# Issuing the first x load of a 2:4 sparse matmul from the ScalarE queue instead of the SyncE queue

## The chip, the cores and the metric

The kernel runs on one core of a Trainium2 chip. The metric is the device time of one execution in microseconds, the median over the runs shown.

## The reference

x has 16 x 512 = 8192 token rows of 1024 values, w is 1024 x 1024, b has 1024 values, all bf16. The rows of w are taken in groups of four along the contraction dimension. In each group and column the two entries of largest magnitude stay and the others become zero (2:4 sparsity); ties at the threshold stay.

```python
G = D // M                                  # M = 4, N = 2
wg = w.reshape(G, M, D)
mag = jnp.abs(wg)
order = jnp.argsort(mag, 1)
thr = jnp.take_along_axis(mag, order[:, M - N:M - N + 1, :], 1)
mask = (mag >= thr).astype(w.dtype)
wp = (wg * mask).reshape(D, D)
return jnp.einsum("bsd,df->bsf", x, wp) + b
```

## The kernel before

The 8192 tokens are 64 tiles of 128. The kernel has two stages.

In the first stage w comes in packed: partition q holds the four rows of group q, so that a group lies in one partition and the mask is elementwise work (`Piece`, L141 to L178: magnitudes, pairwise maxima and minima, threshold, mask, product). w is cut into six pieces (L124): half g of the contraction dimension and a column range. Pieces 0 and 1 are g = 0, columns 0 to 255 and 256 to 511. Since the rows are packed this way, x has to be split the same way, and TensorE transposes it: tiles 0 to 6 of x come in as halves of the contraction dimension ("a" for g = 0, "b" for g = 1), each is transposed in four steps against an identity (`transpose`, L189), and ScalarE copies the result from PSUM to SBUF (`copy_xt`, L198). Then TensorE multiplies with the pruned pieces as they are done (`mm_piece`, L209). The pruned weights also go to a scratch in DRAM and come back in natural row order (`save` L180, `reload` L183).

In the second stage tiles 7 to 63 are loaded with a transposing DMA in batches (`load_batch`, L240) and multiplied with the natural weights (L358 to L403).

The order of work in the first stage is written out by hand, one list per engine (L252 to L268). On TensorE it begins with fillers, matmuls on a tile of zeros whose results are not used: `filler(6, 4)` with 512 columns and `filler(8)` with 128 columns (L342, L343). Then come T6a (transpose tile 6, half a), F5 (five fillers), T5a, T4a, F6, T3a, T2a, F7, M5.0y (tile 5 with the second half of piece 0), and so on; M6.3 is tile 6 with piece 3. Each engine takes its list strictly in order. On VectorE the list is abs0, hi0, lo0, ..., mask0y, mask0x, mult0y, abs1, mult0x, ...: the steps of piece 0, then 1, 3, 2, 4, 5; `mult` is the last step of a piece. On ScalarE it is C6a, C5a, C4a, C2a, C3a, C6b, C1a, abs3, ...: the copies of the transposes, and the magnitudes of later pieces.

The loads of w, x and the bias stand at L104 to L121, all issued from SP in this order: the weights of piece 0 (256 KB), tile 6 half a (128 KB), tiles 4 and 5 half a (256 KB), tiles 2 and 3 half a, the weights of piece 1, and ten more. They run through `issue` (L90), so their instructions have line 92. Between the first two of these calls stands an activation on the tile of zeros (`spark`, L106), whose result is not used; with it the activation table is loaded (ACT_TABLE_LOAD, put there by the compiler).

Of the kernel before, what the change touches and what calls it, by code (L numbers as in the profile page):

```python
# [10 lines left out]
def kernel(  # L11
# [7 lines left out]
    nc = tc.nc  # L19
# [5 lines left out]
    Act = mybir.ActivationFunctionType  # L25
# [35 lines left out]
    def seq(eng, inst):  # L61
        if eng in tails:
            tc.add_manual_dep(inst.ins, tails[eng].ins.name, NOSYNC, reason="program order")
        tails[eng] = inst
        return inst
# [7 lines left out]
    def act(i):  # L73
        return seq("act", i)
# [4 lines left out]
    zeros = const.tile([P, P], bf16)  # L79
    dve(nc.vector.memset(zeros[:], 0.0))  # L80
    spark = const.tile([P, P], bf16)
# [8 lines left out]
    def issue(eng, out_, in_):  # L90
        q = nc.sync if eng == "sp" else nc.scalar
        return seq(eng, q.dma_start(out_, in_))  # L92

    def load_w(g, c0, c1, eng="sp"):
        issue(eng, w_sb[:, g, :, c0:c1], wv[:, g, :, c0:c1])

    def load_x(ta, tb, g, eng="sp"):
        xs = const.tile([P, tb - ta, HK], bf16, name=f"x_{ta}_{g}")
        issue(eng, xs[:], xv[:, ta:tb, g * HK:(g + 1) * HK])
        for t in range(ta, tb):  # L100
            x_sb[(t, g)] = xs[:, t - ta, :]


    load_w(0, 0, 256)  # L104
    for _ in range(1):
        act(nc.scalar.activation(spark[:], zeros[:], Act.Abs))  # L106
    load_x(6, 7, 0)
    load_x(4, 6, 0)
    load_x(2, 4, 0)
    load_w(0, 256, 512)  # L110
# [323 lines left out]
```

## Time and profile before

| | |
|---|---|
| time, median of 4 runs | 236.05 us |
| the four runs | 237.59, 235.97, 235.91, 236.14 us |
| the profiled execution | 237.59 us, of which the span is 235.8 us and 1.79 us lie around it |
| TensorE matmul busy | 230.0 us, 98% of the span |
| VectorE busy | 104.3 us, 44% |
| ScalarE busy | 15.3 us, 7% |
| second stage, matmuls of L395 | 800, 175.4 us, mean 379 ns |
| first stage, matmuls of L220 | 166, 25.4 us |
| transposes L195, fillers L132 | 56 and 32 matmuls, 5.7 and 6.1 us |
| granted TensorE clock in the records | 1.00 |

How to read it: PE is TensorE's matmuls, PEld its weight loads, DVE is VectorE, ACT ScalarE, SPq and ACTq the queues of DMAs that these engines issue. Times count from the start of the span. Matmuls are pipelined, so the duration of one (379 ns) is longer than the spacing of two (219 ns for 512 columns in the second stage). A bracket behind a timeline entry gives the idle time of the engine ahead of it and what ended that. "To landing" is the time from a DMA's issue until its data are there.

### The profile page before, as it was taken

Reading aid. Unit: us, or ns where it says so; the run is one execution under the profiler, and the core shown is the slowest. Engines: PE = TensorE matmul, PEld = TensorE weight load, DVE = VectorE, ACT = ScalarE, POOL = GpSimd, SP = SyncE. Lnnn points to the kernel's source line nnn. Section 1 sums busy time; section 2 is a strip of 40 time slices with the busy share of each in tenths; the row PEclk is TensorE's granted clock in tenths of the full one; section 3 lists DMA queues with packets and bytes.
Section 4 is the critical chain, followed back from the end, with each engine's and each line's share of the span. In section 5 each row is a group of like instructions: output and inputs, shape, how many; then the busy total and the mean of one; then the engine's idle time right before and its main releaser. Section 6 shows DMA issues by size and latency. Waiting matters only on the chain.

```text
span 235.8 us, 2851 instructions
## 1 busy us (share of the span) xinstructions
PE 230.0 (98%) x1164; PEld 114.4 (48%) x1184; DVE 104.3 (44%) x177; ACT 15.3 (7%) x27; POOL 0.7 (0%) x6
## 2 busy tenths in 40 slices
PE   7899999999999999999999999999999999999995
PEld 4899444444444444444444444444444444444443
DVE  3779839733424433432442343344244334324424
ACT  3288300000000000000000000000000000000000
POOL 1000000000000000000000000000000000000000
DMA  5995988999999992794129912496211221222122
GB/s 161 312 328 138 276 304 197 274 268 278 229 320 213 295 246 90 167 258 157 57 76 232 299 50 89 102 283 195 90 74 61 89 92 44 89 89 84 52 89 89
DMA packets 79500, 40.29 MB, mean 171 GB/s; under 512 B 60416, under 2 KB 71936, under 8 KB 79488
## 3 DMA queue, kind: packets, MB, share of 16 engines
q1 hardware_dynamic: 68352, 22.45, 43.6%
q10 hardware_dynamic: 11136, 17.67, 21.8%
q8 instruction: 9, 0.15, 0.3%
q14 instruction: 3, 0.02, 0.0%
HBM read 6.29 MB, written 18.87 MB: 107 GB/s over the span
## 4 chain that ended last, share of the span: by engine, by line
PE 96%; DMA 2%; issue 1%; SPq 1%; DVE 0%
PE ps L395 74%; PE ps L220 10%; PE ps L360 9%; DMA x<-in_x_dram 2%; PE tp L195 2%; PE ps L132 1%; SPq L92 1%; DVE o L364 0%
## 5 line engine op out<-in xcount | busy, mean ns | idle before, releaser
L395 PE MATMUL ps<-wp_nat,xb 128*128 128x512 bf16 x800 | 175.4, 379 | 0.8
L395 PEld LDWEIGHTS <-xb 128*128 128x128 bf16 x816 | 79.8, 98 | 96.3
L364 DVE TENSOR_TENSOR o<-ps,bias_sb 128x512 bf16<-128x512 f32 (+1 forms) x116 | 74.0, 676 | 117.2 <-PE ps L395 106.5
L220 PE MATMUL ps<-wp,xt 128*128 128x256 bf16 (+1 forms) x166 | 25.4, 308 | 0.1
L360 PE MATMUL ps<-wp_nat,xb 128*128 128x512 bf16 (+2 forms) x110 | 21.0, 348 | 0.1
L220 PEld LDWEIGHTS <-xt 128*128 128x128 bf16 x168 | 16.2, 98 | 7.5
L360 PEld LDWEIGHTS <-xb 128*128 128x128 bf16 x112 | 10.4, 98 | 10.7
L132 PE MATMUL ps<-zeros 128*128 128x128 bf16 (+1 forms) x32 | 6.1, 372 | 1.0 <-DVE zeros L80 1.0
L234 DVE TENSOR_TENSOR o<-ps,bias_sb 128x512 bf16<-128x512 f32 x7 | 4.8, 685 | 5.0 <-PE ps L220 5.0
L195 PE MATMUL tp<-ident,x 128*128 128x128 bf16 x56 | 5.7, 252 | 1.1 <-DMA x<-in_x_dram 1.1
L155 ACT ACTIVATE mag<-w_sb 128x1024 bf16<-128x1024 bf16 (+1 forms) x4 | 6.0, 1493 | 0.0
L200 ACT COPY xt<-tp 128x256 f32<-128x256 f32 x14 | 5.0, 373 | 9.2 <-PE tp L195 9.2
L195 PEld LDWEIGHTS <-x 128*128 128x128 bf16 x56 | 4.7, 124 | 1.5 <-DMA x<-in_x_dram 1.4
L152 DVE TENSOR_TENSOR wp<-w_sb,mag 128x1024 bf16<-128x1024 bf16 (+2 forms) x7 | 5.4, 766 | 0.2
L152 DVE TENSOR_TENSOR mag<-mag,hi 128x1024 bf16<-128x1024 bf16 (+2 forms) x7 | 5.3, 767 | 0.2
L132 PEld LDWEIGHTS <-zeros 128*128 128x128 bf16 x32 | 3.7, 147 | 2.6 <-issue 1.7
L235 DVE TENSOR_TENSOR o<-st,bias_sb 128x512 bf16<-128x512 f32 x7 | 4.8, 679 | 0.0
L152 DVE TENSOR_TENSOR lo<-mag 128x512 bf16<-128x512 bf16 (+1 forms) x6 | 3.0, 508 | 1.4 <-ACT mag L155 1.4
L229 ACT COPY st<-ps 128x512 f32<-128x512 f32 x7 | 3.6, 611 | 0.2 <-PE ps L220 0.2
L152 DVE TENSOR_TENSOR hi<-mag 128x512 bf16<-128x512 bf16 (+1 forms) x6 | 3.0, 507 | 0.0
L162 DVE TENSOR_SCALAR mag<-w_sb 128x1024 uint16<-128x1024 uint16 x2 | 0.9, 427 | 4.1 <-DMA w_sb<-in_w_dram 4.1
L152 DVE TENSOR_TENSOR hi<-hi,lo 128x256 bf16<-128x256 bf16 (+1 forms) x6 | 2.0, 337 | 0.2
(11 smaller groups left out, 6.5 us busy)
## 6 DMA issues: line engine op xcount, KB each, us to landing
out_dram<-o ACTq DMA_DIRECT2D x58, 256.0 KB, 4.1
wp_nat<-wp_scratch SPq DMA_DIRECT2D x2, 1024.0 KB, 6.4
x<-in_x_dram SPq DMA_DIRECT2D x5, 256.0 KB, 5.2
out_dram<-o ACTq DMA_DIRECT2D x10, 128.0 KB, 1.7
w_sb<-in_w_dram SPq DMA_DIRECT2D x4, 256.0 KB, 4.9
w_sb<-in_w_dram SPq DMA_DIRECT2D x2, 512.0 KB, 6.3
wp_scratch<-wp SPq DMA_DIRECT2D x4, 256.0 KB, 5.1
wp_scratch<-wp ACTq DMA_DIRECT2D x2, 512.0 KB, 5.0
```

The costliest lines, as they stand in the source:

```text
L132: pe(nc.tensor.matmul(warm_ps[:, :rep * P], lhsT=zeros[:], rhs=zeros[:, None, :].to_broadcast([P, rep, P]), start=True, stop=True))
L152: dve(nc.vector.tensor_tensor(out, a, b_, op=op))
L155: act(nc.scalar.activation(self.mag[:], self.w, Act.Abs))
L195: pe(nc.tensor.transpose(tp[:, m, :], xg[:, m, :], ident[:]))
L200: act(nc.scalar.copy(xt[:].bitcast(fp32), xpk[(t, g)][:].bitcast(fp32)))
L220: pe(nc.tensor.matmul(ps[:, c0 - h * FH:c1 - h * FH], lhsT=xpk[(t, g)][m], rhs=wp[:, g, m, c0:c1], start=(new and m == ms.start), stop=(le ...
L229: act(nc.scalar.copy(st[:], ps_open.pop((t, 0))[:]))
L234: dve(nc.vector.tensor_tensor(o[:, FH:], ps_open.pop((t, 1))[:], bias_sb[:, FH:], op=Alu.add))
L235: dve(nc.vector.tensor_tensor(o[:, :FH], staged.pop(t)[:], bias_sb[:, :FH], op=Alu.add))
L360: pe(nc.tensor.matmul(ps, lhsT=xt[:, kt, :], rhs=wp_nat[:, kt, c0:c1], start=(kt == 0), stop=(kt == KT - 1)))
L364: dve(nc.vector.tensor_tensor(o[:, c0:c1], ps, bias_sb[:, c0:c1], op=Alu.add))
L395: pe(nc.tensor.matmul(pss[h][:], lhsT=xt[:, kt, :], rhs=wp_nat[:, kt, h * FH:(h + 1) * FH], start=(kt == 0), stop=(kt == KT - 1)))
```

## The change

Three lines at the head of the loads. The load of tile 6, half a, is issued from ScalarE's queue and not from SP's, and it stands ahead of the activation, so that on ScalarE it is the first instruction, ahead of the table load. The activation works on one column instead of 128. The loop around it, which ran once, is gone. On SP all following loads stand one place further ahead; nothing else moves on any engine.

```diff
     load_w(0, 0, 256)
-    for _ in range(1):
-        act(nc.scalar.activation(spark[:], zeros[:], Act.Abs))
-    load_x(6, 7, 0)
+    load_x(6, 7, 0, "act")
+    act(nc.scalar.activation(spark[:, :1], zeros[:, :1], Act.Abs))
     load_x(4, 6, 0)
     load_x(2, 4, 0)
     load_w(0, 256, 512)
```

## The prediction

> **What bounds the kernel now.** I read the chain of waits first, since it says which engine the end hangs on. Its columns are start, length and what; times are us from the start of the span.
>
> ```profile
> 1.48 0.60 SPq L92
> 2.08 0.06 issue
> 2.13 4.46 DMA x<-in_x_dram
> 6.60 0.05 issue
> 6.64 1.04 PE tp L195 x8
> 7.68 0.64 PE ps L132 x6
> 8.32 0.85 PE tp L195 x8
> 9.18 0.75 PE ps L132 x7
> 9.92 1.34 PE ps L220 x12
> 11.26 0.45 PE tp L195 x8
> ```
>
> From 6.64 to the last store the chain is TensorE with "issue" pieces of 0.05 us between, so the kernel ends when TensorE ends, and TensorE starts real work when the second x transfer (tiles 4 and 5, 256 KB; "x45" below) lands at 6.60. That transfer is queued on SP behind the first x half tile ("x6"), whose issue is the 0.60 us at 1.48. The second thing to see is pace: eight transposes take 0.85 us at 8.32 and 0.45 us at 11.26. TensorE runs at half pace up to about 9.9 and at full pace after, although the records give the granted clock as 1.00.
>
> The timeline of the first 14 us tells what stands beside this.
>
> ```profile
> 0.74 1.28 ACT L106 ACT_TABLE_LOAD   x1 [0.74 <-PEq L418]
> 0.74 0.68 SPq L92 DMA_DIRECT2D w_sb<-in_w_dram  x1
> 1.48 1.58 SPq L92 DMA_DIRECT2D x<-in_x_dram  x3
> 2.03 0.31 ACT L106 ACTIVATE spark<-zeros 128x128 bf16<-128x128 bf16 x1
> 4.02 0.43 DVE L162 TENSOR_SCALAR mag<-w_sb 128x1024 uint16<-128x1024 uint16 x1 [3.08 <-DMA w_sb<-in_w_dram]
> 4.38 0.63 PE L195 MATMUL tp<-ident,x 128*128 128x128 bf16 x4
> 4.81 0.74 PE L132 MATMUL ps<-zeros 128*128 128x128 bf16 x5
> 5.05 0.37 ACT L200 COPY xt<-tp 128x256 f32<-128x256 f32 x1 [2.71 <-PE tp L195]
> 6.64 1.04 PE L195 MATMUL tp<-ident,x 128*128 128x128 bf16 x8 [1.09 <-DMA x<-in_x_dram]
> 8.16 0.43 DVE L162 TENSOR_SCALAR mag<-w_sb 128x1024 uint16<-128x1024 uint16 x1 [1.06 <-DMA w_sb<-in_w_dram]
> 13.16 0.43 DVE L152 TENSOR_TENSOR lo<-mag 128x512 bf16<-128x512 bf16 x1 [1.39 <-ACT mag L155]
> ```
>
> T6a, the transposes of x6, start at 4.38 with no wait: the fillers ahead of them set that time, and x6 had landed just before (4.31 by the trace's completion records, a slack of 0.07). Then come five fillers, and TensorE is idle until x45. VectorE waits 1.06 us for the second weight piece ("w1", DVE at 8.16) and 1.39 us for ScalarE's magnitude at 13.16. From 13.16 to 28.77 VectorE has no wait left: that is its mask chain, which feeds TensorE piece by piece.
>
> The last view is the busy share of the DMA engines in stretches of 0.5 us (columns: stretch, length, busy time of PE, PEld, DVE, ACT and POOL, granted clock, DMA share, GB/s).
>
> ```profile
> 2.00:2.50 0.50, 0.50 (x3) 0.15 (x1) 0.00 (x0) 0.33 (x2) 0.00 (x0) 1.00 0.38 103
> 2.50:3.00 0.50, 0.50 (x2) 0.15 (x1) 0.00 (x0) 0.00 (x0) 0.00 (x0) 1.00 0.97 278
> 3.00:3.50 0.50, 0.50 (x2) 0.15 (x1) 0.00 (x0) 0.00 (x0) 0.00 (x0) 1.00 1.11 361
> 3.50:4.00 0.50, 0.50 (x6) 0.47 (x5) 0.00 (x0) 0.00 (x0) 0.00 (x0) 1.00 0.83 166
> ```
>
> The engines are part idle only in the first stretch, and full from 2.5 on. Between 3.5 and 4.0 they are full and yet slow, 166 GB/s: single packets of x45 take up to 0.8 us there, and of the sixteen shares of x45 most are in by 5.2, the last two at 6.6.
>
> **What the Trainium skill says.** "TensorE: Matmul & The Clock Gate", Part 1: the array runs at half rate until a busy window of about 3.4 us has passed, the window runs free of the kernel's start, so the moment differs from run to run. The trace agrees on the halves (0.85 against 0.45 us) and shows that TensorE, busy from 0.99 to 5.3, did not switch there, but did at about 9.9. "DMA: Bandwidth & Descriptors", Issuing engines are not separate DMA queues: DMAs from ACT and SP run on the same 16 engines, and a second issuer saves only the sequencer's time; the same page, Queues, rings and completion order: an engine takes turns between the rings that have work. No trace shows ACT and SP loading at once here; a share of 1 from 2.5 on agrees with the first. "ScalarE: Activation LUTs", What ACT_TABLE_LOAD costs: about 1283 ns a load, and 186 ns plus 0.833 ns an element for an ACTIVATE; the trace has 1.28 us and 0.31 us.
>
> **The change part by part.** *SP loses one issue.* x6's issue is 0.65 us of SP (1.48 to 2.13). All later loads move one place up: x45 is issued at 1.48, w1 near 2.45. *ACT gains one issue* ahead of the table load. Two ACT issues at 28.8 take 1.25 us, so 0.62 each; the table load ends near 2.65 instead of 2.02, the small activation near 2.9. It shrinks from 128 columns to 1: 127 x 0.833 = 0.11 us by the skill's price. ACT's next work is the copy at 5.05, so both are hidden with 2.1 us to spare; without that cover they would cost 0.62 - 0.11 = 0.5 us. Nothing else is queued behind the issue.
>
> *x6 itself* is issued near 0.74 instead of 1.48. It can land 0.7 us earlier, and this is worth nothing, because T6a starts behind the fillers. *The first weights* now share the engines with x6. x6 is 128 KB, 0.35 us at the 361 GB/s of the third stretch; at worst w0 lands 0.35 later than 4.0. VectorE would begin at 4.4 and still be ready at 7.5 for w1, which comes at 8.16. Hidden.
>
> *x45 and w1* decide. The bytes ahead of them are the same as before and the engines are full from 2.5 on, so an issue 0.65 us earlier only counts as far as it fills idle engines. Idle in the first stretch: 0.62 x 0.5 = 0.31 us. Bounds: 0.65 us of gain if the landing follows the issue; a loss of 0.2 us if alternating between two rings costs something, which no row prices. I take two thirds of the idle share, 0.2 us, for x45 and for w1 alike.
>
> *What is late next.* Moved ahead by 0.2, TensorE meets the x transfer of tiles 2 and 3 (landing 7.35, wanted at 8.12; it moves too), then the mask chain. The closest meetings are M6.3 at 16.37 against a mult3 that ends at 16.09, and M2.4 about 0.2 us after mult4's end of 23.81. These do not bind, because the mask chain follows: lo3 waits for ScalarE, whose magnitude stands behind a copy of a TensorE transpose. The reload of the pruned weights has over 3 us of slack and moves along.
>
> *From which clock case.* If TensorE had full pace from 6.64 on, its 16 transposes and 13 fillers would take 29 x 0.056 = 1.62 us instead of 3.08: M5.0y would start at 8.26 instead of 9.72, 1.46 earlier. mult0y (7.10), mult0x (8.92 against 9.13) and mult1 (11.77 against 11.84) are then just in time, and the 1.39 us wait of lo3 vanishes: VectorE would run without a wait from w1's landing to the last mask. So such an execution ends about 1.4 us earlier. The profiled execution took 237.59 us, a span of 235.8 and 1.79 around it, and is the slowest of four; the other three have 235.91 to 236.14, 1.45 to 1.68 less. I read it thus: the profiled run switched late, the others early. In an early run TensorE and VectorE both hang on x45 and w1, so 0.2 us counts in full: 236.05 - 0.2 = 235.85. In a late run like the profiled one it is 237.59 - 0.1 to 0.2 = 237.4, since time gained at half pace counts half if the switch stays put.
>
> **The rivals.** *First: all runs switch early, and those of before did not.* If the 1.6 us between the profiled and the other runs is the price of recording, the shown median is a late-switch time, and a shorter idle stretch (5.34 to 6.4 instead of 6.64, or less if x45's slow packets go too) lets the clock rise early: 236.05 - 1.46 - 0.2 = 234.4. For it: three runs agree within 0.23 us, which a free-running window hardly gives. Against it: the 1.6 us fits the replay too well.
>
> *Second, the slower side: x6 comes late.* T6a has 0.07 us of slack. If ACT's first DMA starts slower than SP's, or x6 waits out w0 and part of x45 on the shared engines, and lands after about 4.7, TensorE stands idle between 4.4 and 4.7 and again before x45; the busy stretch 0.99 to 5.34 is broken after 3.4 us, and most runs keep half pace until about 9.9. Then 1.46 us comes on top: 237.5. For it: the thin slack; against it: ACT and SP are both free at 0.74, and x6 has half of the bytes of w0 or x45.
>
> *Third: nothing moves.* The engines are full, x45's slow packets are what they were, and 236.05 stays; or the slow packets go and x45 and w1 land early. What that can bring is capped by VectorE, which is busy with the first piece to 7.10: 8.16 - 7.10 = 1.06, so 235.0. Both are within the bound of "no change".
>
> **How the numbers follow.** A half per cent, 1.18 us, is about what a measurement of this kernel can tell from no change. Forecast, 235.85 with its own range 235.4 to 236.25 (the bounds +0.2 and -0.65): 0.42. Third rival, 235.0 to 236.05: 0.16. First rival, 234.4 (0.2 either way): 0.24. Second, 237.5: 0.18. So faster 0.24, same 0.58, slower 0.18. The range leaves out only the second rival: 234.3 to 236.5.
>
> **What would show it.** In the profile after: x6's issue under ACT at 0.74, the table load behind it, x45 issued near 1.5 (all sure); T6a still at 4.38 without a wait (second rival: a wait on x there); x45's end in the chain at 6.4 (nothing moves: 6.6); VectorE's second wait on w shorter by 0.2; and the pace of the transposes behind x45, 0.056 or 0.107 us apiece, which tells early from late. Wrong would be the forecast if runs of the kernel before spread over both clock cases evenly, or if x45 landed a microsecond sooner or later.

## The result and the profile after

| | before | after |
|---|---|---|
| median | 236.08 us (55 runs) | 235.47 us (34 runs) |
| lowest and highest | 235.31 and 238.2 us | 234.91 and 236.9 us |
| runs of 236.9 us and more | 9 of 55 | 1 of 34 |
| profiled execution, span | 237.59 and 235.8 us | 235.23 and 233.4 us |

The ratio of the times is 0.9969, with a 95% interval of 0.9957 to 0.9982: faster by 0.3%, clear of 1, though less than the half per cent that the prediction took as the limit of what a measurement can tell. The forecast was 235.85. In every ratio here, a run more than 1.5% above the fastest of its kernel is left out (two in all, both in experiments), while the medians take in every run.

Without the runs of 236.9 us and more the medians are 236.00 (46 runs) and 235.43 (33 runs), 0.57 apart. So nearly all of the 0.61 us stands between ordinary runs and does not come from fewer late ones.

The two profiled executions differ by 2.4 us, four times the median's difference, and must not be read as the effect: the one of before has the array at half pace up to 9.9 us, the one of after up to 4.4. This is the chain of waits of after (start, length, what).

```profile
1.49 3.98 DMA x<-in_x_dram
5.47 0.05 issue
5.51 0.64 PE tp L194 x8
6.15 0.34 PE ps L131 x6
6.49 0.56 PE tp L194 x8
7.05 0.39 PE ps L131 x7
7.44 1.31 PE ps L219 x12
8.75 0.45 PE tp L194 x8
```

It still starts at x45's landing, but that is issued at 1.49 instead of 2.13 and lands at 5.47 instead of 6.60. Behind it eight transposes take 0.45 to 0.64 us, never 0.85 or 1.04: full pace from x45 on. The timeline of after shows the parts of the change.

```profile
0.73 0.39 ACTq L92 DMA_DIRECT2D x<-in_x_dram  x1
0.73 0.69 SPq L92 DMA_DIRECT2D w_sb<-in_w_dram  x1
1.15 1.28 ACT L106 ACT_TABLE_LOAD   x1 [1.15 <-PEq L417]
2.45 0.20 ACT L106 ACTIVATE spark<-zeros 128x1 bf16<-128x1 bf16 x1
3.87 0.43 DVE L161 TENSOR_SCALAR mag<-w_sb 128x1024 uint16<-128x1024 uint16 x1 [2.94 <-DMA w_sb<-in_w_dram]
4.37 0.42 PE L194 MATMUL tp<-ident,x 128*128 128x128 bf16 x4
6.93 0.43 DVE L161 TENSOR_SCALAR mag<-w_sb 128x1024 uint16<-128x1024 uint16 x1
10.64 0.42 DVE L151 TENSOR_TENSOR lo<-mag 128x512 bf16<-128x512 bf16 x1
```

T6a starts at 4.37 without a wait, as before. The first weights are not late (3.87, before 4.02). VectorE's second wait for weights is gone: at 6.93 it goes straight on from the first piece, where it started at 8.16 before. And the step at 10.64 (lo3, the first step of piece 3), which had waited 1.39 us for ScalarE at 13.16, now waits 0.1 us.

How such a start goes with the end can be seen across the profiles: the last mask product (mult5) ends at 28.78 before and 26.27 after, and the spans, 235.8 and 233.4, lie 207.0 and 207.1 us behind it. In the twelve experiments they lie 207.0 to 207.6 behind it, so the end of VectorE's mask chain tells the end of the kernel to about half a microsecond.

This does not make the mask chain the cause. In both profiles here TensorE, once x45 has landed, waits for no mask. The two engines are tied both ways: TensorE multiplies with what VectorE has finished, and lo3 takes ScalarE's magnitude (which ends at 13.12 before and 10.61 after), and that stands behind ScalarE's copies of TensorE's transposes. Of the 2.51 us between 28.78 and 26.27, 1.23 are the earlier start on the second weights (8.16 to 6.93) and 1.3 the shorter wait of lo3, which belongs to the late pace of TensorE. That splits the time and not the causes, since in both profiles lo3 starts when ScalarE is done.

### The profile page after: what moved, and what is told of

Same layout as the page of the kernel before. It is cut to its first block, busy times and chain, and to the rows that moved or that the text cites. A ratio compares the mean times of both kernels' runs of the same rounds, so it can differ in the third digit from the quotient of the medians.

```text
span 233.4 us, 2851 instructions
## 1 busy us (share of the span) xinstructions
PE 228.3 (98%) x1164; PEld 112.6 (48%) x1184; DVE 104.1 (45%) x177; ACT 15.1 (6%) x27; POOL 0.7 (0%) x6
## 4 chain that ended last, share of the span: by engine, by line
PE 96%; DMA 2%; issue 1%; SPq 0%; DVE 0%
PE ps L394 75%; PE ps L219 10%; PE ps L359 9%; DMA x<-in_x_dram 2%; PE tp L194 1%; PE ps L131 0%; SPq L92 0%; DVE o L363 0%
## 5 line engine op out<-in xcount | busy, mean ns | idle before, releaser
L359 PEld LDWEIGHTS <-xb 128*128 128x128 bf16 x112 | 10.4, 98 | 10.7
L131 PE MATMUL ps<-zeros 128*128 128x128 bf16 (+1 forms) x32 | 5.1, 320 | 1.0 <-DVE zeros L80 1.0
L194 PE MATMUL tp<-ident,x 128*128 128x128 bf16 x56 | 4.7, 220 | 0.4 <-DMA x<-in_x_dram 0.4
L194 PEld LDWEIGHTS <-x 128*128 128x128 bf16 x56 | 4.1, 114 | 0.7 <-DMA x<-in_x_dram 0.6
L131 PEld LDWEIGHTS <-zeros 128*128 128x128 bf16 x32 | 2.8, 118 | 2.6 <-issue 1.7
```

Of the source, the lines that this page charges most:

```text
L131: pe(nc.tensor.matmul(warm_ps[:, :rep * P], lhsT=zeros[:], rhs=zeros[:, None, :].to_broadcast([P, rep, P]), start=True, stop=True))
L194: pe(nc.tensor.transpose(tp[:, m, :], xg[:, m, :], ident[:]))
L359: pe(nc.tensor.matmul(ps, lhsT=xt[:, kt, :], rhs=wp_nat[:, kt, c0:c1], start=(kt == 0), stop=(kt == KT - 1)))
```

## The experiments

My theory after the result: the loads behind tile 6 land earlier, and the clock is a lottery beside it. Open was what brings the loads forward: the issue slot freed on SP, or the bytes of tile 6 flowing earlier on a ring of their own; and whether the short activation or the clock's moment is the gain. "Slot" below is SP's time for one issue: with it freed, x45 is issued at 1.49 instead of 2.13 and the second weights at 2.63 instead of 3.10. Ratios are to runs of the kernel before taken beside each experiment, with 95% intervals. Landings are by the trace's completion records.

### The move alone, and the activation alone

```diff
 # e1_move_only, from the changed kernel
-    act(nc.scalar.activation(spark[:, :1], zeros[:, :1], Act.Abs))
+    act(nc.scalar.activation(spark[:], zeros[:], Act.Abs))
 # e2_spark_only, from the kernel before
-        act(nc.scalar.activation(spark[:], zeros[:], Act.Abs))
+    act(nc.scalar.activation(spark[:, :1], zeros[:, :1], Act.Abs))
```

> The changed kernel with the small activation back at 128 columns; the load of tile 6 stays on ScalarE's queue. Theory (the gain is that the loads behind tile 6 on SP land earlier): 235.5, as the changed kernel. Rival (the shorter activation matters): part of the gain goes, 235.8 or more.

> The kernel before with the activation at 1 column and nothing else. Theory: 236.1, no change, since ScalarE waits 2.7 us before its first copy anyway. Rival (the shorter activation matters): 235.8 or less.

Measured: 235.28 us (11 runs, ratio 0.9975, 0.9966 to 0.9984) for the move alone; 236.19 (22 runs, 1.0005, 0.9984 to 1.0025) for the activation alone, beside 236.07 before. The move brings the whole gain without the short activation, and the short activation alone brings none that its interval shows.

### Tile 6 on ScalarE's queue, behind the activation

```diff
-    load_x(6, 7, 0, "act")
     act(nc.scalar.activation(spark[:, :1], zeros[:, :1], Act.Abs))
+    load_x(6, 7, 0, "act")
```

> Tile 6 on ScalarE's queue, but behind the table load and the activation, so issued near 2.2 instead of 0.73. SP has the same free slot as in the changed kernel. If the gain is SP's slot alone, the transfer of tiles 4 and 5 still lands near 5.5. Tile 6 then shares the engines with it and lands near 4.8 to 5.2, after the 4.37 at which TensorE wants it, so TensorE stops twice. Theory: the early landing gains 0.6, the stop costs up to 0.6, and the full pace comes late in more runs: 235.8 to 236.5, with more runs above 237. Rival (the place on ScalarE's queue is indifferent): 235.5.

Measured: 235.71 us (14 runs, 0.9985, 0.9966 to 1.0004). The expectation was wrong in its premise, as the timeline of this kernel shows:

```profile
0.73 1.28 ACT L105 ACT_TABLE_LOAD   x1 [0.73 <-PEq L417]
0.97 0.40 ACTq L92 DMA_DIRECT2D x<-in_x_dram  x1
2.03 0.21 ACT L105 ACTIVATE spark<-zeros 128x1 bf16<-128x1 bf16 x1
4.38 0.63 PE L194 MATMUL tp<-ident,x 128*128 128x128 bf16 x4
```

The load is issued at 0.97, while the table load runs and before the activation that precedes it in the program. Tile 6 lands in time, T6a waits for nothing, and x45 still lands at 5.51. So this run did not test a late tile 6. What the place ahead of the table load is worth stays open: the median lies 0.24 us above the changed kernel's and 0.43 above that of the move alone, which ran beside it, but the intervals overlap.

### SP's slot taken again

```diff
     act(nc.scalar.activation(spark[:, :1], zeros[:, :1], Act.Abs))
+    slot = const.tile([16, 64], bf16, name="slot")
+    sp(nc.sync.dma_start(slot[:], b.rearrange("(p o) -> p o", o=64)))
     load_x(4, 6, 0)
```

> The changed kernel with a 2 KB load (the bias as 16 rows of 128 bytes, not used by anything) in the place on SP that tile 6 had: SP's issue slot is taken again, the bytes are not. Theory (SP's slot decides): the loads behind it are issued 0.6 us later again and most of the gain goes, 235.9 to 236.1. Rival (tile 6's bytes on a ring of their own, beside the first weights, decide): 235.5.

Measured: 235.99 us (14 runs, 1.0013, 0.9988 to 1.0039), beside 236.07 before. The gain is gone, though tile 6 is issued at 0.73 and lands at 3.01, as in the changed kernel (0.73 and 3.05). The windows of the first loads show where (columns: stretch, length, busy time of PE, PEld, DVE, ACT and POOL, granted clock, DMA share, GB/s). First the changed kernel:

```profile
1.50:2.00 0.50, 0.50 (x3) 0.19 (x2) 0.00 (x0) 0.50 (x1) 0.00 (x0) 1.00 0.36 43
2.00:2.50 0.50, 0.50 (x3) 0.15 (x1) 0.00 (x0) 0.49 (x2) 0.00 (x0) 1.00 0.90 266
...
3.50:4.00 0.50, 0.50 (x6) 0.48 (x5) 0.13 (x1) 0.00 (x0) 0.00 (x0) 1.00 0.72 252
4.00:4.50 0.50, 0.50 (x8) 0.50 (x6) 0.47 (x2) 0.00 (x0) 0.00 (x0) 1.00 0.87 293
4.50:5.00 0.50, 0.50 (x10) 0.40 (x8) 0.50 (x2) 0.17 (x1) 0.00 (x0) 1.00 0.88 303
```

Then the kernel with the slot taken:

```profile
1.50:2.00 0.50, 0.50 (x3) 0.19 (x2) 0.00 (x0) 0.50 (x1) 0.00 (x0) 1.00 0.21 68
2.00:2.50 0.50, 0.50 (x3) 0.15 (x1) 0.00 (x0) 0.49 (x2) 0.00 (x0) 1.00 0.81 259
...
3.50:4.00 0.50, 0.50 (x6) 0.48 (x5) 0.17 (x1) 0.00 (x0) 0.00 (x0) 1.00 0.88 66
4.00:4.50 0.50, 0.50 (x8) 0.50 (x6) 0.47 (x2) 0.00 (x0) 0.00 (x0) 1.00 0.85 182
4.50:5.00 0.50, 0.50 (x7) 0.50 (x6) 0.50 (x3) 0.00 (x0) 0.00 (x0) 1.00 0.83 248
```

Both flow from 1.75 or so, half a microsecond ahead of the kernel before. But from 3.5 to 4.5 the second falls to 66 and 182 GB/s with the engines as busy as ever. The kernel before has this slow stretch too (166 from 3.5 to 4.0, and these two), and the changed kernel does not:

```profile
4.00:4.50 0.50, 0.50 (x8) 0.47 (x7) 0.45 (x2) 0.00 (x0) 0.00 (x0) 1.00 1.02 207
4.50:5.00 0.50, 0.50 (x7) 0.50 (x6) 0.50 (x2) 0.00 (x0) 0.00 (x0) 1.00 0.85 256
```

The landings say it less sharply than the times. In this profile, an execution of 235.76 us and thus one of the faster of its kernel, x45 lands at 5.90 and the second weights at 7.34, about halfway between the kernel before (6.60 and 8.13) and the changed one (5.47 and 6.91).

### Early bytes without the slot, and the slot without early bytes

```diff
 # e9_swap_sp, from the kernel before
+    load_x(6, 7, 0)
     load_w(0, 0, 256)
     ...
-    load_x(6, 7, 0)
     load_x(4, 6, 0)
 # e10_merge, from the kernel before
-    load_x(6, 7, 0)
-    load_x(4, 6, 0)
+    load_x(4, 7, 0)
```

> The kernel before, all on SP, with tile 6 issued ahead of the first weights. Tile 6's issue is short (0.39 us on ScalarE's queue) and its packets follow 0.6 us after it, so data flow from 1.75 instead of 2.2, and tile 6's bytes fill that stretch; no slot on SP is saved (tiles 4 and 5 stay at 2.13). Theory (the early flow of tile 6 is the larger part of the gain): the second weights land near 7.3 instead of 7.9, 235.6 to 235.8. Rival (the slot freed on SP is the gain): 236.1. The first weights land 0.3 to 0.5 later, which the wait of VectorE on the second weights hides.

> The kernel before, all on SP, with tiles 4, 5 and 6 in one load of 384 KB: one issue fewer on SP as in the changed kernel, but the first data still flow only from 2.2, and tile 6 comes only with tiles 4 and 5, near 6. TensorE stands idle from 4.38 until then. Theory (early flow decides, the slot alone is worth little): the second weights land near 7.6 to 7.9; TensorE is about 0.5 later and the full pace comes late in most runs, 236.5 to 237.5. Rival (the slot decides): the second weights land near 7.0 even so.

Measured: 236.05 us (22 runs, 1.0, 0.9981 to 1.0019) with tile 6 first on SP, and 235.93 (14 runs, 0.9997, 0.9972 to 1.0023) with the merged load, beside 236.28 before. In the first, data do flow from 1.75 and x45 lands at 5.29, but it brings nothing: the x tiles behind it land at 7.20, and VectorE takes the second weights at 8.11.

```profile
5.34 0.85 PE L195 MATMUL tp<-ident,x 128*128 128x128 bf16 x8
7.25 0.64 PE L195 MATMUL tp<-ident,x 128*128 128x128 bf16 x8 [0.72 <-DMA x<-in_x_dram]
8.11 0.43 DVE L162 TENSOR_SCALAR mag<-w_sb 128x1024 uint16<-128x1024 uint16 x1 [0.70 <-DMA w_sb<-in_w_dram]
```

As a test of early flow this run is weak, because its flow thins out behind tile 6 (118 GB/s from 2.5 to 3.0) and by 3.0 it has read no more than the kernel before, 190 kB. The run with the slot taken is the better one: about 310 kB by 3.0, and no gain. In the second kernel the data start as late as before, and VectorE takes the second weights at 6.77, without a wait:

```profile
6.77 0.42 DVE L161 TENSOR_SCALAR mag<-w_sb 128x1024 uint16<-128x1024 uint16 x1
```

Its windows:

```profile
2.00:2.50 0.50, 0.50 (x3) 0.15 (x1) 0.00 (x0) 0.33 (x2) 0.00 (x0) 1.00 0.37 104
...
3.50:4.00 0.50, 0.50 (x6) 0.47 (x5) 0.23 (x1) 0.00 (x0) 0.00 (x0) 1.00 1.07 373
4.00:4.50 0.50, 0.50 (x6) 0.32 (x4) 0.47 (x2) 0.00 (x0) 0.00 (x0) 1.00 1.09 383
4.50:5.00 0.50, 0.09 (x1) 0.00 (x1) 0.50 (x3) 0.00 (x0) 0.00 (x0) 1.00 1.09 381
```

From 3.5 to 5.0 it moves 373 to 383 GB/s where the kernel before has 166 to 256. So the theory behind both expectations, early flow, fell. Its rival, the slot, holds for the landings; the median of the merged load does not show it. Adding up each window's GB/s times 0.5 us from 1.5 to 5.0 gives what had been read by 5.0: about 690 kB before, 710 with tile 6 first on SP, 650 with the slot taken; 860 in the changed kernel and 910 with the merged load. The merged load's time shows less of this because tile 6 now comes with tiles 4 and 5: T6a starts at 5.00 instead of 4.38, and 3 of its 14 runs have 237.1 us or more. The other 11 have a median of 235.64, where the 45 runs of before under 236.9 have 236.12, but no interval says that this kernel is faster.

### The clock

```diff
 # e6_before_cold, from the kernel before
-    filler(6, 4)
-    filler(8)
 # e5_before_bridge, from the kernel before; e7_after_bridge, from the changed kernel
-            "T6a F5 T5a T4a F6 ...
+            "T6a F17 T5a T4a F6 ...
```

> The kernel before without the 14 fillers at the start (6 of 512 and 8 of 128 columns, whose results nothing uses), so TensorE begins at 4.3 with tile 6 and can't reach full pace before the transposes. Theory: nearly every run is like the slow group of before or worse, 237.5 to 238.5. Rival (the slow group isn't the clock): 236.1.

> The kernel before with 17 instead of 5 fillers behind T6a, so that TensorE stays busy from 0.99 until about 6.6 at half pace (12 x 0.107 = 1.28 us against an idle time of 1.3). The work is the same. Theory (runs above 237 are those in which the switch to full pace comes only near 9.9, because of the idle stretch): no run above 237, median 236.0. Rival (the slow group has another cause): a sixth of the runs above 237 as before. If the long filler train delays the transposes in runs with quick transfers, the median rises by 0.1 to 0.3.

> The changed kernel with 17 instead of 5 fillers behind T6a. At full pace they take 17 x 0.056 = 0.95 us from 4.63, until 5.58, about the landing of tiles 4 and 5 (5.5). Theory: the slow group (4 runs of 34 at 236.45 to 236.9) goes, the median stays at 235.5 or rises by 0.1. Rival: the slow group stays.

Without the first fillers: 237.9 us, 236.03 to 239.77 (22 runs, ratio 1.0036, 1.001 to 1.0062), beside 236.27. The loads land as before (x45 at 6.27), only the pace differs; 18 of 22 runs have 236.9 us or more, 18 of 67 before. Its timeline:

```profile
6.32 1.04 PE L195 MATMUL tp<-ident,x 128*128 128x128 bf16 x8 [0.72 <-DMA x<-in_x_dram]
7.79 1.06 PE L195 MATMUL tp<-ident,x 128*128 128x128 bf16 x8
9.39 1.96 PE L220 MATMUL ps<-wp,xt 128*128 128x256 bf16 x12
11.19 0.61 PE L195 MATMUL tp<-ident,x 128*128 128x128 bf16 x8
```

So the moment of full pace is worth a microsecond or more. The profiles agree with the prediction's reading of the four times: the three with full pace only from about 10 us are of executions of 237.59 to 238.06 us, the eleven with an earlier one of 235.23 to 236.07. Not all late runs need be of one kind, though: in 8 of the 41 runs of before at 236.9 us and more that stand beside the experiments, the records give a granted clock of 0.992 or 0.993, in the rest of them 0.999 or 1.00.

The bridging fillers did not do what I expected. In the kernel before: 236.32 us (22 runs, 0.9999, 0.9982 to 1.0016), three runs above 237, of 22, where before has 18 of 67; too few to tell. In the changed kernel it is 236.19 (14 runs, 0.9995, 0.9966 to 1.0023), and six of 14 runs have 236.7 or more: the gain of the median is gone, though the interval does not exclude a part of it. That 17 fillers at half pace take 17 x 0.107 = 1.82 us from 4.8 to 6.6, past x45's landing near 5.1 to 5.5, would do this; no profile caught such a run, so it is argued.

### More on ScalarE's queue

```diff
 # e8_two_on_act, from the changed kernel
     load_x(6, 7, 0, "act")
+    load_x(4, 6, 0, "act")
     act(nc.scalar.activation(spark[:, :1], zeros[:, :1], Act.Abs))
-    load_x(4, 6, 0)
 # e11_split_w, from the changed kernel (load_w takes a range of m)
-    load_w(0, 0, 256)
+    load_w(0, 0, 256, "sp", 0, 2)
+    load_w(0, 0, 256, "act", 2, 4)
     load_x(6, 7, 0, "act")
```

> The changed kernel with tiles 4 and 5 also issued from ScalarE's queue, ahead of the table load; SP goes on with tiles 2 and 3 and the second weights straight behind the first. Issue of tiles 4 and 5 near 1.15 instead of 1.49, all else on SP 0.55 us earlier still. Theory: the engines are full from 2.0 on, so tiles 4 and 5 gain at most 0.3, but the first weights share the engines with 384 KB instead of 128 and land up to 0.5 later, and VectorE, which in the changed kernel runs without a wait from those weights on, follows them: 235.4 to 236.0. Rival (each issue slot freed on SP is worth another 0.6): 234.9.

> The changed kernel with the first weights in two halves, one from SP and one from ScalarE's queue ahead of tile 6: both issues are short, so both halves flow from about 1.75, and tiles 4 and 5 are issued on SP near 1.2. In the changed kernel VectorE works without a wait from the first weights on, so an earlier landing of these (3.4 instead of 3.85) should carry on to the last mask. Theory: 235.0 to 235.2. Rival (the second weights or the loads behind them bind in most runs): 235.5.

> The changed kernel once more, beside the three others on the same chip: 235.5, with a tenth of the runs near 236.8.

Measured: 235.88 us with two loads on ScalarE's queue (22 runs, 0.9974, 0.9957 to 0.9991), 235.61 with the first weights split (14 runs, 0.9977, 0.9955 to 1.0), 235.45 for the changed kernel again (22 runs, 0.9957, 0.9937 to 0.9978, beside 236.28). Neither beats the changed kernel. With two loads the first weights share the engines and VectorE is late at once:

```profile
4.91 0.43 DVE L161 TENSOR_SCALAR mag<-w_sb 128x1024 uint16<-128x1024 uint16 x1 [3.98 <-DMA w_sb<-in_w_dram]
7.91 0.42 DVE L161 TENSOR_SCALAR mag<-w_sb 128x1024 uint16<-128x1024 uint16 x1
8.05 1.14 PE L219 MATMUL ps<-wp,xt 128*128 128x256 bf16 x9 [0.71 <-DVE wp L151]
```

It starts at 4.91 instead of 3.87 and never gets that back; even TensorE waits for it. The split brings VectorE forward, to 3.42 and 6.63, but tile 6 now stands behind half the weights, and the time is given back on the other side:

```profile
4.97 0.41 PE L195 MATMUL tp<-ident,x 128*128 128x128 bf16 x4 [0.51 <-DMA x<-in_x_dram]
10.67 0.42 DVE L152 TENSOR_TENSOR lo<-mag 128x512 bf16<-128x512 bf16 x1 [0.43 <-ACT mag L155]
```

T6a waits for tile 6, the transposes and ScalarE's magnitude behind them come no earlier, and VectorE waits for that at 10.67, the very place that it reached at 10.64 in the changed kernel.

## Why the prediction was right, and what it mis-sized

**What bounds it, and through what.** Right for what the profiles of before and after show: the chain hangs on x45, and from there TensorE works to the end without waiting for a mask. That x45 and the second weights both count in an early execution fits two runs. With tile 6 first on SP, x45 landed at 5.29 and the time did not fall, while the x tiles behind it (7.20) and the second weights (taken at 8.11) were as late as before. With the bridging fillers in the kernel before (235.97 us), the end of mult1, which follows the second weights, and the end of ScalarE's magnitude, which follows TensorE's start on x45, stand together, at 11.37 and 11.38.

**What costs nothing.** Right on each count: ScalarE's later table load (ended at 2.43, its next work at 4.83), the shorter activation (the two runs of its own), tile 6's own earlier landing (2.89 with tile 6 first on SP, and no gain), the first weights sharing the engines (3.85, before 4.00). ScalarE's issue took 0.39 us, not 0.62.

**The size for x45 and the second weights.** This is the term that failed: 0.2 us was forecast, from engines "full from 2.5 on". In the two profiles x45 lands 1.1 us earlier (6.60 to 5.47) and VectorE takes the second weights 1.2 earlier (8.16 to 6.93). With three more profiles that have the loads of before (7.76 to 7.85 for the second weights) and four more with those of the changed kernel (6.92 to 7.32), the averages are 1.1 for x45 (6.36 to 5.28) and 0.8 for the second weights. The prediction named an x45 that lands a microsecond sooner as a sign that it was wrong, and for this term it was.

A share of 0.8 to 1 of busy engines did not mean that they moved data at their rate. The filling of idle engines was sized well: by 3.5 the changed kernel has read about 430 kB against 370, 60 kB, which is 0.17 us at the prediction's 361 GB/s. What the forecast left out is that the slow stretch between 3.5 and 5.0, which I had pointed out, would go with the slot: 424 kB against 315 there. My upper bound of 0.65 us was too low for a landing, as the slow packets go as well, though the second weights were issued only 0.47 earlier, at 2.63 and not near 2.45. From 3.5 to 5.0 the trace has 11 to 18 packets of x that take over 0.25 us in the kernel before, in its three profiles with the same loads and in the one with the slot taken, and 0 to 3 in the five profiles with the loads of the changed kernel. Why packets are slow there when SP has one issue more among its first loads is open. The runs show that the slot decides it, not by what mechanism, and they do not part the time of the issue from the number of loads ahead.

**What is late next.** In part. The cap that I gave the third rival, VectorE's first piece to about 7.1, is where the second weights now end: no wait at 6.93. And lo3, which I took to follow, becomes a limit of its own: it stands 0.09, 0.28, 0.40 and 0.49 us behind the end of mult1, waiting for ScalarE's magnitude, in the four profiles with the loads and fillers of the changed kernel. In the two with the longest waits, ScalarE itself had waited for the weights of piece 3, so there a load further back in SP's queue is the limit:

```profile
10.25 1.06 ACT L154 ACTIVATE mag<-w_sb 128x1024 bf16<-128x1024 bf16 x1 [0.42 <-DMA w_sb<-in_w_dram]
```

This is the changed kernel measured again. As an estimate, 0.8 less the mean wait of 0.32 is 0.5 us, beside a median that moved by 0.61. That the median of 235.47 still lies inside the forecast's own range (235.4 to 236.25), by 0.07 us, is in part luck: the landings gained more than its bound, and lo3 took some of it back.

**The clock cases.** The reading of the four times is borne out: the profiled run of before switched late, the profiled executions near 236 us early, and runs of the kernel with no first fillers spread over 3.7 us with unchanged loads. The first rival, in which the change makes full pace come early in all runs where before it did not, is excluded: the median moved by 0.61 and not 1.66. Its smaller form, fewer late runs, is there but not settled: 9 of 55 runs at 236.9 or more before; 1 of 34, and 1 of 22 when measured again, after. Since all runs are 0.6 earlier, some of these only slip below the line: with the line at 236.3 it is 4 of 34 and 3 of 22 after.

**The second rival**, tile 6 late, did not come: it lands at 3.05. The one run meant to force it did not, but the split of the first weights did: tile 6 at 4.93, T6a waiting 0.51 us. The late pace that the prediction priced at 1.46 us did not follow: that profile has full pace from 5.1, and 13 of its 14 runs have 235.86 or less.

**The third rival** had two halves. Nothing moves is excluded by the interval. The other, that the slow packets go and x45 and the second weights land early, is what the profiles show; the time of 235.47 lies halfway between its cap of 235.0 and no change.

## What to carry to other kernels

A queue's issue time at the head of a kernel can be part of the critical path even where the DMA engines look full; judge by GB/s per stretch, and test with a tiny load in the freed slot. A profile of one execution cannot price a change of half a microsecond when the array's clock rises at another moment in each run: compare many runs, with and without the late group, and read several profiles for what moved. Before moving more onto the second queue, look at what then stands behind what: each of the two further moves here delayed one first piece at least as much as it advanced another.

## What the runs showed of the hardware

- A DMA that follows a table load and an activation on ScalarE was issued 0.24 us into the 1.28 us of the table load, before the activation ran: the order in the program did not hold the DMA back.
- The first load on a queue sent its first packets 0.6 to 1.1 us after its issue ended: in the changed kernel tile 6 (128 KB in 128 rows, issue 0.39 us from 0.73) at 1.75, the whole first weights (512 rows, issue 0.69 us from 0.73) at 2.2 to 2.4 in the kernels that begin with them, and their half on ScalarE's queue (issue 0.51 us from 0.73) at 2.36.
- Sixteen DMA engines with a busy share of 0.88 moved 66 GB/s in one stretch and, with 1.09, 383 GB/s in another, on loads of the same tensors.
- The twelve experiments and the two kernels show full pace from moments between 3.6 and 6.5 us in eleven profiles and near 10 in three (9.9 to 10.4), while the granted clock in the records is 1.00 in all of these stretches.
